# Layer 2's first stage in slots of one block product, part of its weight preparation in layer 1, and the last stage's sums on VectorE

## The chip, the cores and the metric

The kernel runs on one core of a Trainium2 chip. The metric is the device time of one execution in microseconds. The kernel before takes 1717.92 us, the median of three runs (1717.18 to 1718.33).

## The reference

Pooled attention is followed by two MLPs, all in float32; the second layer's product is where most of the change lies.

```python
k_p, v_p = k.mean over 8 rows, v.mean over 8 rows          # 8 batches, 8 heads, 576 x 64
x = softmax(q @ k_p.T / 8) @ v_p                            # -> 4608 tokens x 512
h = x @ w_in1;  y = (h * sigmoid(h)) @ w_out1               # 512 -> 2048 -> 512
h = y @ w_in2;  g = h * clip(h + 3, 0, 6) / 6;  out = g @ w_out2
```

## The kernel before

The 4608 tokens are cut into 9 groups of 512. The order of the instructions on every engine is the order in which the program issues them, and each engine works its queue in that order. All transfers between HBM and SBUF are issued by SP, in program order too.

**Layer 1 with attention** comes first: 9 groups of 16 steps, a step being one block of 128 hidden features (`h_mm`, then `y_mm` of the step before). Beside it the attention of the next group is computed, and the weights of layer 2 are prepared. Float32 products are made of three matmuls on a high part and a low part, so every operand is split: ScalarE makes the high part, GpSimd or VectorE the difference.

**Layer 2** uses a scheme of seven block products in place of eight. Both operands, cut into 2 x 2 blocks, are replaced by seven sums of blocks each. The *preparation* of a weight matrix is done in 8 pairs of feature blocks, and for each pair: four quarter blocks are loaded (`load_half`) and converted from their float64 words (`half_a`: one ScalarE and three VectorE instructions); GpSimd forms four sums (`combine`); seven results are split (`half_b`: ScalarE and GpSimd) and stored to HBM (`ws`). `factor_jobs(piece)` deals this out in seven jobs a pair. In layer 1 a job is begun in those steps of groups 1 to 7 for which `SPLITTING` has a one (9 of 16). There `w_in2` (piece 0) is prepared; `w_out2` (piece 1) is prepared in layer 2's first stage, by `work`, called at three of the seven products (at one of them every second time).

**The first stage of layer 2** walks over 36 values of `e` (9 groups of tokens times 4 double blocks of features). Each `e` has seven block products, numbered k, in the order 0, 4, 3 of the `e` before, 5, 2 of the `e` before, 1, 6; the first `e` has five and two are left at the end, 252 in all. A product is 12 matmuls of 256 columns (`product`, L639). Products 0, 5, 6 and 3 add up in one PSUM bank, 4 and 2 in another, and the running sum is read out in between (L1024, L1034 on ScalarE; L1027, L1039 on VectorE), so that TensorE cannot add product 5 before product 0 has been read. Four products of an `e` end in a *gate* (`relu6`): ScalarE's Relu (L654), then VectorE's minimum and product (L656) into a tile `go`, which is stored to HBM (`g2`, L658). The store is put on a list, `later`, and issued when the next `e` begins. `go` has four buffers. The seven sums of the next group's x are made by `make_x` (GpSimd sum, ScalarE high part, GpSimd low part), from four blocks that `load_x1` loads two `e` ahead.

In the last four `e`, `last_factor` loads the prepared blocks of `w_out2` (512 KB each, 28 in all) into places that the last products have freed, and `load_g` the first group's gates (8 of 512 KB).

**The last stage** has 9 groups of seven products of 48 matmuls each (`last_product`, L712). `sums` forms the sums of g on GpSimd (L206, `gr<-gr`, 8 of 1024 columns a group), `split_g` splits the next product's operand (ScalarE L698, VectorE L699), and the results are added up by `summed` (VectorE, L1063) and, twice a group, by `combine` on GpSimd.

Of the kernel before, what the change touches and what calls it, by code (L numbers as in the profile page):

```python
# [20 lines left out]
GT = 512  # L21
# [4 lines left out]
def kernel(  # L26
# [152 lines left out]
    def half_a(f, piece, a):  # L179
        raw = half_raw.pop((f, piece, a))  # L180
        hw = raw[:, :, 1]
        mag = prep_tile("mag", [P, HW], F32)
        bits = mag.bitcast(U32)
        nc.scalar.activation(mag, hw.bitcast(F32), AF.Copy, scale=2.0 ** -112)
# [11 lines left out]
        half_mag[f, piece, a] = mag  # L196

    def half_b(mag, dst):

        t = prep_tile("out", [P, 2, HW], F32R)  # L200
        nc.scalar.activation(t[:, 0], mag, AF.Copy)  # L201
        nc.gpsimd.tensor_tensor(out=t[:, 1], in0=mag, in1=t[:, 0].bitcast(F32), op=ALU.subtract)  # L202
# [12 lines left out]
    def pair_jobs(p, piece, rest):  # L215
        d, j = divmod(p, 2)
        f = 2 * p
        m = half_mag
        a11, a12, a21, a22 = (
            ((f, 0, 0), (f, 0, 1), (f + 1, 0, 0), (f + 1, 0, 1)),  # L220
            ((f, 1, 0), (f + 1, 1, 0), (f, 1, 1), (f + 1, 1, 1)),
        )[piece]
# [360 lines left out]
    def open_late():  # L583
# [3 lines left out]
        prep.update(raw=(own, "raw", 3), mag=(own, "mag", 4), out=(own, "out", 4))  # L587
# [20 lines left out]
    def make_x(g, i):  # L608

        k = MADE[i]  # L610
        b11, b12, b21, b22 = (x_raw[a, b] for a in range(2) for b in range(2))
        src = (b11, b11, b11, b12, b21, b21, b22)[i]
# [6 lines left out]
        elif i == 5:  # L619
            combine(ALU.subtract, b21, b21, b11)  # L620
        t = late["x"][(7 * g + i) % 9]
        nc.scalar.activation(t[:, 0], src, AF.Copy)  # L622
        nc.gpsimd.tensor_tensor(out=t[:, 1], in0=src, in1=t[:, 0].bitcast(F32), op=ALU.subtract)  # L623
        x_st[g, k] = t.rearrange("p a (c n) -> p a c n", c=2)
# [26 lines left out]
    def relu6(h, g, d, fh, th):  # L651

        t = new_f32("t", "t")
        nc.scalar.activation(t, h, AF.Relu, scale=1.0 / 6.0, bias=half)  # L654
        o = new_f32("o", "go")
        nc.vector.scalar_tensor_tensor(out=o, in0=t, scalar=1.0, in1=h, op0=ALU.min, op1=ALU.mult)  # L656
        dst = g2[g][:, fh, th, 2 * d:2 * d + 2, :]
        later.append(lambda: nc.sync.dma_start(out=dst, in_=o.rearrange("p (j n) -> p j n", j=2)))  # L658
# [19 lines left out]
    def sums(g, k):  # L678
# [3 lines left out]
        for dd in range(2):  # L682
            b11, b12, b21, b22 = (g_in[g, a, b, dd] for a in range(2) for b in range(2))
            if k == 4:
                combine(ALU.subtract, b11, b12, b11)
            elif k == 6:
                combine(ALU.subtract, b12, b22, b12)
            elif k == 5:
                combine(ALU.subtract, b11, b22, b11)
            else:  # L690
                combine(ALU.subtract, b21, b21, b11)
# [57 lines left out]
    with tc.manual_schedule():  # L749
# [100 lines left out]
        SPLITTING = (0, 1, 0, 1, 0, 1, 1, 1, 0, 1, 0, 1, 0, 1, 1, 0)  # L850
        jobs = list(factor_jobs(0))
# [105 lines left out]
        jobs = list(factor_jobs(1))  # L957
        ahead2 = [key for key, _ in jobs if key]
        jobs_b = []

        def work(n):

            nonlocal jobs_b
            for _ in range(n):
                for job in jobs_b:
                    job()
                jobs_b = []
                if jobs:
                    key, jobs_b = jobs.pop(0)
                    if key:  # L970
                        half_a(*key)
                    while ahead2 and len(half_raw) < 3:
                        load_half(*ahead2.pop(0))

        while len(half_raw) < 3:
            load_half(*ahead2.pop(0))
        n_all = NG * ND
        xs_, zs, kept = {}, {}, {}
        freed = []
        wanted = [(d, k) for k in LAST for d in range(ND)]  # L980

# [4 lines left out]
        for e in range(n_all + 1):  # L986
            g, d = divmod(e, ND)
            due, later[:] = list(later), []
            for job in due:
                job()  # L990
            if e == n_all - ND:
                while jobs or jobs_b:
                    work(1)
                for job in later:
                    job()
                later.clear()
# [3 lines left out]
            if n_all - ND < e:  # L1000
                while freed:
                    last_factor()
                for _ in range(4):
                    if g_next[0] < 10 and g_next[0] < 8:
                        n = g_next[0]
                        load_g(0, *G_ORDER[n // 2], n % 2)
            if g + 1 < NG and d == 1:
                load_x1(g + 1)
            for ee, k in steps_of(e, n_all):
                gg, dd = divmod(ee, ND)  # L1010
                if k == 0:
                    xs_[ee] = ps_h.tile([P, GT], F32, tag="h", name="px")
                elif k == 4:
                    zs[ee] = ps_a.tile([P, GT], F32, tag="a", name="pz")
                ps = {0: xs_, 5: xs_, 6: xs_, 3: xs_, 4: zs, 2: zs}.get(k, {}).get(ee)
                if ps is None:
                    ps = ps_y.tile([P, 512], F32, tag=f"y{ee % 2}", name="py")
                product(ps, gg, dd, k, k in (0, 4, 1))
                if gg == NG - 1:
                    freed.append(tag_of[0, dd, k])  # L1020
                ph = column_sets(ps)
                if k in (0, 5, 6):
                    t = kept[ee, k] = new_f32({0: "gh", 5: "gl"}[k], f"c{k}") if k != 6 else late["pool"].tile([P, GT], F32, tag="u3", name="u3")
                    nc.scalar.activation(in_sets(t), ph, AF.Copy)  # L1024
                    if k == 6:
                        u4 = late["pool"].tile([P, GT], F32, tag="u4", name="u4", bufs=1)
                        nc.vector.tensor_tensor(  # L1027
                            out=in_sets(u4), in0=in_sets(t), in1=column_sets(zs[ee]), op=ALU.add
                        )
                        kept.pop((ee, 6))  # L1030
                        relu6(u4, gg, dd, 1, 1)
                elif k == 3:
                    t = late["pool"].tile([P, GT], F32, tag="u3", name="u3")
                    nc.scalar.activation(in_sets(t), ph, AF.Copy)  # L1034
                    relu6(t, gg, dd, 1, 0)
# [130 lines left out]
```

## Time and profile before

| What | Value |
|---|---|
| Median of 3 runs | 1717.92 us |
| Profiled execution, its own time | 1716.91 us |
| Its span (first to last instruction) | 1715.0 us |
| Mean granted TensorE clock | 0.978 |
| TensorE matmul busy | 1591.8 us (93%) |
| VectorE, ScalarE, GpSimd busy | 1089.2, 702.2, 677.0 us |
| Attention and layer 1 | 0 to 887 us |
| First stage of layer 2 | 887 to 1356 us |
| Last stage | 1356 to 1715 us |

Times in the profile are in microseconds from the span's start; "mean ns" is the duration of one instruction. PE is TensorE, PEld its weight loads, DVE VectorE, ACT ScalarE, POOL GpSimd, SPq the queue of SP, which issues the transfers. An entry such as `go<-t,c` names the tile written and those read. `<-` before an engine or DMA names what ended an idle time.

### The profile page before, as it was taken

The page shows a single profiled execution, that of the slowest core. Times are in us where ns is not written, and L with a number is a line of the kernel's source. Part 1 is how long each engine was busy: PE and PEld are TensorE (multiplying, and loading weights), DVE is VectorE, ACT ScalarE, POOL GpSimd, SP SyncE. Part 2 cuts the span into 40 slices and gives each one's busy share as a digit, 9 for nine tenths or more (in the row PEclk, how much of TensorE's full clock was granted, in tenths as well). Part 3 has the DMA queues.
Part 4 walks back from the last instruction along what each step waited for, and adds up shares of the span by engine and source line. Part 5 has one row for each costly group of instructions (what it writes and reads, how often), then busy time and mean ns, then how long its engine had stood idle before and what let it go on. Part 6 is the DMA issues. An engine that isn't in the chain of part 4 may idle for free.

```text
span 1715.0 us, 26954 instructions
## 1 busy us (share of the span) xinstructions
PE 1591.8 (93%) x10510; PEld 1429.4 (83%) x10510; DVE 1089.2 (64%) x1457; ACT 702.2 (41%) x1208; POOL 677.0 (39%) x523
## 2 busy tenths in 40 slices
PE   7899999999999999999998776788998699999998
PEld 6466888888888888888898775778898699999998
DVE  7996655656656565544235545546444588888887
ACT  5443553333333333332235445455554334434333
POOL 4633441212121212100215345445332377767676
PEclk9999999999999999999999999989999899999999
DMA  9342333333334343212545453644335943344441
GB/s 294 140 153 72 113 109 120 124 125 110 109 97 140 111 139 110 94 51 87 211 161 173 167 178 121 216 166 166 142 130 227 381 130 123 125 138 132 146 146 47
DMA packets 119711, 245.42 MB, mean 143 GB/s; under 512 B 12448, under 2 KB 38944, under 8 KB 119584
## 3 DMA queue, kind: packets, MB, share of 16 engines
q1 hardware_dynamic: 119584, 243.71, 41.9%
q8 instruction: 82, 1.34, 0.3%
q14 instruction: 45, 0.37, 0.1%
HBM read 146.67 MB, written 96.99 MB: 142 GB/s over the span
## 4 chain that ended last, share of the span: by engine, by line
PE 56%; DVE 15%; issue 12%; POOL 7%; DMA 5%; ACT 5%; SPq 0%; POOLq 0%; ACTq 0%; DVEq 0%
PE hps L502 20%; PE y L560 20%; DVE gs L699 8%; PE pl L712 8%; PE px L639 2%; POOL xst L623 2%; POOL xr L206 2%; PE aps L467 2%; ACT t L654 2%; PE aps L363 2%; POOL hout L202 1%; DMA g<-go 1%; PE pz L639 1%; ACT gs L698 1%; PE y L543 1%
## 5 line engine op out<-in xcount | busy, mean ns | idle before, releaser
L502 PE MATMUL hps<-x,whl 128*128 128x512 f32 x1728 | 402.1, 382 | 4.2 <-POOL whl L155 2.1
L502 PEld LDWEIGHTS hps<-x,whl 128*128 128x128 f32 x1728 | 326.1, 189 | 56.2 <-issue 5.4
L712 PE MATMUL pl<-wst,gs 128*128 128x256 f32 x3024 | 348.0, 277 | 12.4 <-DVE gs L699 6.8
L712 PEld LDWEIGHTS pl<-wst,gs 128*128 128x128 f32 x3024 | 342.6, 193 | 17.9 <-DVE gs L699 12.3
L560 PE MATMUL y<-gh,whl 128*128 128x512 f32 x1024 | 310.1, 384 | 0.0
L699 DVE TENSOR_TENSOR gs<-gr,gs 128x1024 fp32r<-128x1024 f32 x126 | 282.6, 2287 | 23.4 <-ACT gs L698 23.4
L639 PE MATMUL px<-xst,wst 128*128 128x256 f32 x1728 | 227.8, 288 | 64.6 <-ACT u L1024 38.9
L639 PEld LDWEIGHTS px<-xst,wst 128*128 128x128 f32 x1728 | 211.6, 200 | 77.3 <-ACT u L1024 44.3
L202 POOL TENSOR_TENSOR hout<-hmag,hout 128x256 fp32r<-128x256 f32 x112 | 87.8, 784 | 460.7 <-ACT hout L201 436.7
L206 POOL TENSOR_TENSOR gr<-gr 128x1024 f32<-128x1024 f32 x72 | 238.8, 3351 | 63.0 <-DVE gs L699 57.2
L522 DVE SCALAR_TENSOR_TENSOR hps<-t,hps 128x512 f32<-128x512 f32 x128 | 88.3, 690 | 217.7 <-ACT t L521 217.3
L560 PEld LDWEIGHTS y<-gh,whl 128*128 128x128 f32 x1024 | 189.5, 189 | 29.6 <-issue 4.1
L521 ACT ACTIVATE t<-hps 128x512 f32<-128x512 f32 x128 | 76.4, 597 | 297.4 <-PE hps L502 295.8
L560 PE MATMUL y<-gl,whl 128*128 128x512 f32 x512 | 194.1, 379 | 0.0
L698 ACT ACTIVATE gs<-gr 128x1024 fp32r<-128x1024 f32 x126 | 127.4, 1055 | 147.8 <-PE pl L712 104.2
L623 POOL TENSOR_TENSOR xst<-xr,xst 128x512 fp32r<-128x512 f32 x63 | 81.3, 1292 | 255.3 <-ACT xst L622 172.3
L531 DVE TENSOR_TENSOR gl<-hps,gh 128x512 fp32r<-128x512 f32 x128 | 88.5, 691 | 86.0 <-ACT gh L530 86.0
L656 DVE SCALAR_TENSOR_TENSOR go<-t,u 128x512 f32<-128x512 f32 x72 | 54.6, 758 | 137.5 <-ACT t L654 76.0
L639 PE MATMUL pz<-xst,wst 128*128 128x256 f32 x864 | 117.1, 289 | 22.7 <-DVE c L1039 22.7
L639 PEld LDWEIGHTS pz<-xst,wst 128*128 128x128 f32 x864 | 109.5, 203 | 25.1 <-DVE c L1039 25.0
L530 ACT ACTIVATE gh<-hps 128x512 fp32r<-128x512 f32 x128 | 76.6, 599 | 115.4 <-DVE hps L522 115.4
L654 ACT ACTIVATE t<-c,half 128x512 f32<-128x512 f32 x72 | 52.0, 722 | 149.6 <-DVE c L1039 149.5
(104 smaller groups left out, 1783.5 us busy)
## 6 DMA issues: line engine op xcount, KB each, us to landing
g<-go SPq DMA_DIRECT2D x144, 256.0 KB
gr<-g SPq DMA_DIRECT2D x72, 512.0 KB
ws<-hout SPq DMA_DIRECT2D x112, 256.0 KB
wst<-ws SPq DMA_DIRECT2D x56, 512.0 KB
bl<-bT SPq DMA_DIRECT2D x28, 384.0 KB
x<-o SPq DMA_DIRECT2D x36, 256.0 KB
xr<-x SPq DMA_DIRECT2D x36, 256.0 KB
wraw<-in_moe_w_in_dram SPq DMA_DIRECT2D x16, 512.0 KB
```

Of the source, the lines that this page charges most:

```text
L202: nc.gpsimd.tensor_tensor(out=t[:, 1], in0=mag, in1=t[:, 0].bitcast(F32), op=ALU.subtract)
L206: nc.gpsimd.tensor_tensor(out=out, in0=a, in1=b, op=op)
L502: nc.tensor.matmul(ps, w[:, c, :], shuffled(x[:, c, :]), start=(c == 0 and n == 0), stop=(c == NKC - 1 and n == 2),)
L522: nc.vector.scalar_tensor_tensor(out=ps, in0=t, scalar=1.0, in1=ps, op0=ALU.add, op1=ALU.mult)
L531: nc.vector.tensor_tensor(out=in_two(gl), in0=dealt(ps), in1=in_two(gh).bitcast(F32), op=ALU.subtract)
L560: nc.tensor.matmul(ps, a, shuffled(b), start=(f == 0 and n == 0), stop=(f == NF - 1 and n == 2),)
L623: nc.gpsimd.tensor_tensor(out=t[:, 1], in0=src, in1=t[:, 0].bitcast(F32), op=ALU.subtract)
L639: nc.tensor.matmul(ps[:, j * HW:(j + 1) * HW], w[:, j, a, c, :], shuffled(x[:, b, c, :]), start=(first and j == 0 and n == 0 and c == 0), ...
L654: nc.scalar.activation(t, h, AF.Relu, scale=1.0 / 6.0, bias=half)
L698: nc.scalar.activation(t[:, dd, 0], src, AF.Copy)
L699: nc.vector.tensor_tensor(out=t[:, dd, 1], in0=src, in1=t[:, dd, 0].bitcast(F32), op=ALU.subtract)
L712: nc.tensor.matmul(ps[:, c * HW:(c + 1) * HW], t[:, dd, a, i, c * P:(c + 1) * P], shuffled(w[:, b]), start=(dd == 0 and c == 0 and i == 0 ...
```

## The change

**Layer 1.** `factor_jobs` takes no piece now: it deals out all 8 pairs of `w_in2` and then the first four (`EARLY`) of `w_out2`, 85 jobs in place of 57, and `SPLITTING` has 14 ones in 16.

**First stage of layer 2.** The loop runs over a flat list of the 252 products, called slots. The remaining four pairs of `w_out2` are cut into single steps (`pair_steps`: one conversion on ScalarE, one on VectorE, one high part, one low part, or one sum), 104 in all, and one step is issued in every second slot. `half_a` and `half_b` are cut in two for that. A gate of slot n issues its Relu in slot n + 1, its VectorE product in n + 2 and its store in n + 3, each behind that slot's own copy or add. The Relu writes straight into the tile that is stored, and this tile rotates over six buffers (two of tag `t`, four of tag `o`). The steps of `make_x` are dealt out over slots in the same way by a table, `XPLAN`, and `load_x1` is issued in the fourth slot of its `e`.

**Last stage.** The sums run on VectorE, behind the split of the next product's operand and no longer ahead of it, and so do the two additions a group that were left on GpSimd.

```diff
     def half_a(f, piece, a):
+        half_scale(f, piece, a)
+        half_bits(f, piece, a)
...
-    def factor_jobs(piece):
+    EARLY = 4
+    def factor_jobs():
         rest = []
-        for p in range(NF // 2):
-            yield from pair_jobs(p, piece, rest)
+        for piece, n in ((0, NF // 2), (1, EARLY)):
+            for p in range(n):
+                yield from pair_jobs(p, piece, rest)
...
+    def pair_steps(p, piece, last):
...
+        return [
+            scale(a22), *first, scale(a21), bits(a22), scale(a11), bits(a21), head(3, a22),
+            tail(3, a22), make(ALU.add, a22, a21, a22), bits(a11), scale(a12), head(4, a22),
...
+        ], [head(2, a22), tail(2, a22)]
...
-        prep.update(raw=(own, "raw", 3), mag=(own, "mag", 4), out=(own, "out", 4))
+        prep.update(raw=(own, "raw", 3), mag=(own, "mag", 5), out=(own, "out", 4))
...
-                combine(ALU.subtract, b11, b12, b11)      # and three more, in sums()
+            nc.vector.tensor_tensor(out=to, in0=a, in1=b, op=ALU.subtract)
...
-        SPLITTING = (0, 1, 0, 1, 0, 1, 1, 1, 0, 1, 0, 1, 0, 1, 1, 0)
+        SPLITTING = (0, 1, 1, 1, 1, 1, 1, 1, 1, 1, 1, 1, 0, 1, 1, 1)
...
+        slots = [(e, ee, k) for e in range(n_all + 1) for ee, k in steps_of(e, n_all)]
...
+        def gate(n, h, g, d, fh, th):
+            o = new_f32("too"[n_gates[0] % 3], "go")
...
+            at(n + 1, relu)
+            at(n + 2, product_of)
+            at(n + 3, store)
+
+        XPLAN = {
+            (2, 0): ("h", 0), (2, 1): ("t", 0), (2, 2): ("s", 1), (2, 4): ("h", 1), (2, 5): ("t", 1),
...
+            (4, 6): ("t", 5), (5, 0): ("h", 6), (5, 1): ("t", 6),
+        }
...
+            for job in coming.pop(n, ()):
+                job()
...
+            if d == 1 and pos == 3 and g + 1 < NG:
                 load_x1(g + 1)
...
+            if steps and n % 2 and e < n_all - ND:
+                steps.pop(0)()
...
         for n, (g, k) in enumerate(seq):
+            if n + 1 < n_last:
+                split_g(*seq[n + 1])
             if k in ADDS:
                 sums(g, ADDS[k])
-            if n + 1 < n_last:
-                split_g(*seq[n + 1])
...
-                combine(ALU.add, s42, s42, u2)
+                nc.vector.tensor_tensor(out=s42, in0=s42, in1=u2, op=ALU.add)
```

## Rows read from the trace of the kernel before

**Rows 1.** The page: TensorE's busy tenths in 40 slices of 42.9 us.

```profile
PE   7899999999999999999998776788998699999998
```

**Rows 2.** Busy time by stage: PE, PEld, DVE, ACT, POOL, clock, DMA share, GB/s.

```profile
166.00:887.00 721.00, 721.00 (x3789) 625.13 (x3788) 400.52 (x739) 251.78 (x476) 147.01 (x175) 1.00 0.36 119
887.00:1205.00 318.00, 249.33 (x1948) 238.16 (x1948) 172.94 (x255) 162.29 (x311) 149.39 (x147) 0.93 0.48 168
1205.00:1309.00 104.00, 98.34 (x844) 95.21 (x843) 51.45 (x70) 60.25 (x101) 40.01 (x32) 1.00 0.35 127
...
1310.00:1366.00 56.00, 37.15 (x283) 35.90 (x282) 24.36 (x28) 19.48 (x29) 8.44 (x3) 0.85 1.03 403
1356.00:1715.00 359.00, 348.02 (x3024) 342.58 (x3024) 310.04 (x171) 135.46 (x144) 262.00 (x90) 0.99 0.40 133
```

**Rows 3.** TensorE's weight loads in order of time: start, duration, tiles, count.

```profile
886.84 1.52 PEld L639 LDWEIGHTS px<-xst,wst 128*128 128x128 f32 x12
...
1309.76 1.42 PEld L639 LDWEIGHTS pz<-xst,wst 128*128 128x128 f32 x12
1311.10 1.42 PEld L639 LDWEIGHTS py<-xst,wst 128*128 128x128 f32 x12
```

**Rows 4.** The chain of work that ended last, from 1700 us: start, us, what.

```profile
1699.99 11.29 PE pl L712 x101
```

**Rows 5.** Who waited for whom, 890 to 1205 us: total, times, longest.

```profile
DVE go L656 <- DMA g<-go: 40.1, 11, 6.6
...
PE px L639 <- ACT u L1024: 27.9, 17, 2.3
...
PE pz L639 <- DVE c L1039: 20.8, 11, 4.3
PE px L639 <- ACT c L1024: 20.0, 24, 3.3
```

**Rows 6.** The same stretch, waits of SP's queue.

```profile
SPq L176 <- DVE hmag L192: 136.7, 22, 16.1
```

**Rows 7.** SP's issues in order of time, first stage of layer 2.

```profile
1227.38 1.95 SPq L603 DMA_DIRECT2D xr<-x  x4
...
1268.22 1.96 SPq L603 DMA_DIRECT2D xr<-x  x4
...
1309.06 2.39 SPq L252 DMA_DIRECT2D wst<-ws  x5
```

**Rows 8.** The end of the first stage in order of time; idle time before in brackets.

```profile
1325.32 0.69 DVE L656 SCALAR_TENSOR_TENSOR go<-t,u 128x512 f32<-128x512 f32 x1 [7.52 <-DMA g<-go]
...
1341.83 0.69 DVE L656 SCALAR_TENSOR_TENSOR go<-t,u 128x512 f32<-128x512 f32 x1 [9.52 <-DMA g<-go]
...
1353.18 0.69 DVE L656 SCALAR_TENSOR_TENSOR go<-t,u 128x512 f32<-128x512 f32 x1 [4.36 <-DMA g<-go]
...
1356.22 0.80 PE L712 MATMUL pl<-wst,gs 128*128 128x256 f32 x2 [5.39 <-ACT gs L698]
```

**Rows 9.** Busy time on the preparation's tile `hmag` by stage: DVE, ACT, POOL.

```profile
166.00:887.00 721.00, 47.51 (x96) 40.12 (x88) 63.90 (x88) 1.00 0.36 119
887.00:1205.00 318.00, 63.33 (x96) 34.60 (x88) 70.59 (x87) 0.93 0.48 168
```

**Rows 10.** VectorE's differences of the last stage: duration, min/median/max in ns.

```profile
L699 DVE TENSOR_TENSOR gs<-gr,gs x126: 1209/2070/3403, 1356.3 to 1703.6; 128x1024 fp32r<-128x1024 f32 x126
```

**Rows 11.** The last stage in order of time, around 1480 to 1511 us.

```profile
1478.03 23.29 POOL L206 TENSOR_TENSOR gr<-gr 128x1024 f32<-128x1024 f32 x7
1479.09 3.40 DVE L699 TENSOR_TENSOR gs<-gr,gs 128x1024 fp32r<-128x1024 f32 x1
...
1502.92 2.35 DVE L699 TENSOR_TENSOR gs<-gr,gs 128x1024 fp32r<-128x1024 f32 x2
1505.21 0.69 DVE L1063 TENSOR_TENSOR u<-c,pl 128x512 f32<-128x512 f32 x1
```

**Rows 12.** Who waited for whom, 1356 to 1715 us: total, times, longest.

```profile
PE pl L712 <- DVE gs L699: 6.8, 18, 0.5
```

More of the change, by code (lines that the diff above doesn't have):

```diff
@@ L606, with x_blocks, x_sum @@
     MADE = (0, 4, 5, 6, 1, 3, 2)
[L608 to L612, printed above, removed]
+    def x_blocks():
+        return [x_raw[a, b] for a in range(2) for b in range(2)]
+    def x_sum(i):
+        b11, b12, b21, b22 = x_blocks()
         if i == 1:
@@ L649, in new_f32, with late_f32 @@
         return p2.tile([P, GT], F32, tag=tag, name=name, bufs=4 if tag == "o" else 2)
[L651 to L658, printed above, removed]
+    def late_f32(tag, name, bufs=2):
+        return late["pool"].tile([P, GT], F32, tag=tag, name=name, bufs=bufs)
     G_ORDER = ((0, 0), (1, 0), (0, 1), (1, 1))
@@ L955 @@
         make_x(0, 6)
[L957 to L976, printed above, removed]
+        steps = []
+        last = []
+        for p in range(EARLY, NF // 2):
+            now, last = pair_steps(p, 1, last)
+            steps += now
+        steps += last
+        ahead2 = [
+            q[i] for p in range(EARLY, NF // 2) for q in (quarters(p, 1),) for i in (3, 2, 0, 1)
+        ]
         n_all = NG * ND
+        slots = [(e, ee, k) for e in range(n_all + 1) for ee, k in steps_of(e, n_all)]
         xs_, zs, kept = {}, {}, {}
@@ L984, in last_factor, with at, relu, product_of @@
             load_factor(1, d, k, freed.pop(0))
-        for e in range(n_all + 1):
-            g, d = divmod(e, ND)
[L988 to L996, printed above, removed]
+        def at(n, job):
+            coming.setdefault(n, []).append(job)
+        n_gates = [0]
+        def gate(n, h, g, d, fh, th):
+            o = new_f32("too"[n_gates[0] % 3], "go")
+            n_gates[0] += 1
+            def relu():
+                nc.scalar.activation(o, h, AF.Relu, scale=1.0 / 6.0, bias=half)
+            def product_of():
+                nc.vector.scalar_tensor_tensor(
+                    out=o, in0=o, scalar=1.0, in1=h, op0=ALU.min, op1=ALU.mult
+                )
+            def store():
+                nc.sync.dma_start(
+                    out=g2[g][:, fh, th, 2 * d:2 * d + 2, :], in_=o.rearrange("p (j n) -> p j n", j=2)
+                )
+            at(n + 1, relu)
+            at(n + 2, product_of)
+            at(n + 3, store)
+        XPLAN = {
[4 rows of a table added]
+        }
+        def x_job(what, g, i):
+            if what == "s":
+                x_sum(i)
+            elif what == "h":
+                x_head(g, i)
+            else:
+                x_tail(g, i)
+        while len(half_raw) < 3:
+            load_half(*ahead2.pop(0))
+        e_now, pos = -1, 0
+        n = -1
+        total = len(slots)
+        for n, (e, ee, k) in enumerate(slots):
+            g, d = divmod(e, ND)
+            e_now, pos = e, pos + 1 if e == e_now else 0
+            if pos == 0 and e == n_all - ND:
+                while steps:
+                    steps.pop(0)()
+                while later:
+                    later.pop(0)()
                 late["prep"].close()
@@ new lines @@
+            for job in coming.pop(n, ()):
+                job()
+            for of, q in ((d, g + 1), (d + ND, g)):
+                if (of, pos) in XPLAN and 0 < q < NG:
+                    what, i = XPLAN[of, pos]
+                    x_job(what, q, i)
+            if d == 1 and pos == 3 and g + 1 < NG:
+                load_x1(g + 1)
+            if steps and n % 2 and e < n_all - ND:
+                steps.pop(0)()
+                while ahead2 and len(half_raw) < 3:
+                    load_half(*ahead2.pop(0))
@@ L1052 @@
+            while later:
+                later.pop(0)()
+        for m in range(total, total + 4):
+            for job in coming.pop(m, ()):
+                job()
         while freed and wanted:
             last_factor()
-        for job in later:
-            job()
-        later.clear()
+        assert not coming and not wanted
         n_last = NG * 7
@@ L1111 @@
                 s4 = kept.pop("s4")
-                combine(ALU.add, s4, s4, u3)
+                nc.vector.tensor_tensor(out=s4, in0=s4, in1=u3, op=ALU.add)
                 store(g, 1, 1, s4)
```

160 lines of the change are left out of this document (93 added, 67 removed), and 2 rows, old and new, of the table XPLAN.

## The prediction

> **What bounds the kernel now.** I read the page's slices first, then busy times by stage, the waits of each stretch, and the timeline where a wait is long. In the slices TensorE is full in layer 1 and in the last stage, and has holes between, in the first stage of layer 2 [rows 1]. By stage: from 166 to 887 us TensorE is busy in all of the 721.0 us, and no other engine in more than 401. From 887 to 1205 us, while w_out2 is prepared, it is busy 249 of 318 us; from 1205 to 1309, preparation done, 98 of 104; from 1310 to 1366, 37 of 56; in the last stage 348 of 359 [rows 2].
>
> The price of one product without holes is the distance of two neighbours, 1311.10 - 1309.76 = 1.34 us, or 0.112 us a matmul [rows 3]. The last stage agrees: 11.29 / 101 = 0.112 [rows 4]. The first stage has 252 products, 337.7 us of work, and took 1356.2 - 886.8 = 469.4 [rows 3, 8]. So 131.7 us are to be had there at most, in three parts.
>
> (a) The preparation. TensorE waits there for sums to be read out: 27.9 + 20.0 us for ScalarE's copies, 20.8 for VectorE's adds [rows 5]. Neither engine is full, 162 and 173 of 318 us [rows 2]; they are late because their queues are in order. One chain stands out. SP waits 136.7 us in 22 goes, up to 16.1, for a conversion to free a raw buffer [rows 6]; the stores of gates queue behind it; so VectorE waits 40.1 us for a `go` buffer [rows 5], and the adds and Relus behind that wait for VectorE.
>
> (b) 1205 to 1309 us. A group of 28 products takes 1268.22 - 1227.38 = 40.84 us, and the next, up to 1309.06, the same [rows 7]: 1.459 a product, 0.12 over the price.
>
> (c) The hand-over from 1309. The DMA engines are saturated, 403 GB/s from 1310 to 1366 us, 22.6 MB [rows 2]. VectorE waits three times for a store that stands behind the loads, 7.52, 9.52 and 4.36 us [rows 8].
>
> **Layer 1, four pairs more.** This is half of what `hmag` shows for one weight matrix. At layer 1's prices, half of 47.5, 40.1 and 63.9: 24 us on VectorE, 20 on ScalarE, 32 on GpSimd [rows 9], with 16 loads and 28 stores. All are dealt out over 721 us in which ScalarE has 469 idle and GpSimd 574 [rows 2]; TensorE's work, without a gap there although 57 jobs already ran beside it, hides them. Price 0; without that cover, all of ScalarE's, +20.
>
> **The first stage, slots 0 to 228** (up to the 34th e, where the loads of w_out2 begin). They took 1309.06 - 886.84 = 422.2 us [rows 3, 7], 1.844 each. What is left per slot: on ScalarE 60.25 us in 104, or 0.845 per product of 1.459, and half of 34.6 over 229 slots, 0.08: 0.92. VectorE: 0.72 + 0.14 = 0.86. GpSimd: 0.56 + 0.15 = 0.71 [rows 2, 9]. All stay below 1.34, so if order alone made the holes, TensorE sets the pace. The order now has a copy ahead of a Relu whose add came a slot earlier, and every copy has two products' time, 2.7 us, before TensorE needs it. SP waits for at most one conversion just issued, and a gate's buffer comes round after six gates, some ten slots, 14 us, where the longest of the old waits was 6.6 [rows 5]. What is late next: the first block of x is loaded four slots, 5.4 us, before ScalarE wants it; its four loads are issued in 2 us [rows 7] and at 403 GB/s the 1.05 MB move in 2.6, so it just fits; then the last low part of x, on GpSimd, about a product ahead of its use. Bounds for the slot: 1.34, all holes gone, and 1.459, the old pace without preparation. I take 1.37, a quarter of the way, since what made 1.459 was order and the order is what is edited. 229 x 1.37 = 313.7: a gain of 108.5 us (bounds 115.3 and 88.1).
>
> **The hand-over.** Bytes and issue order of the loads stay: 9 loads of 512 KB, then 11, 7, 9. At 403 GB/s such a load takes 1.30 us, a store of 256 KB 0.65. This explains the old waits: 9 loads, four stores, 11 loads and a store are 11.7 + 2.6 + 14.3 + 0.65 = 29.3 us from 1310, or 1339.3; the wait ended at 1341.83 [rows 8], so a landing comes 2.5 us behind its turn. In the new order stores are issued one by one, three of the four of an e behind the next e's loads, and the wait moves from VectorE to ScalarE's Relu, which now writes the stored buffer; queued behind it are ScalarE's copies, and TensorE waits for those after three products. The last Relu's buffer is freed by the twelfth store: 27 loads and 12 stores, 35.1 + 7.8, with 1 us of start and 2.5 of landing 46.4 us after the loads begin. From the end of the old last wait to the last stage's first matmul it is 1356.22 - 1353.18 = 3.0 [rows 8]. So the last stage starts at about +49, against 1356.22 - 1309.06 = 47.2 now: no gain, +2. Two buffers more, and a place later in the queue, cancel. Bounds: 23 products at 1.34 and the old last idle time of 5.4 [rows 8], 36 us (-11), and +6 if the stalls add up.
>
> The Trainium skill, DMA: Bandwidth & Descriptors, section Queues, rings and completion order, says that completion is not in order of issue, so that a later transfer may finish first. By that the stores could pass the loads and the stage would end as TensorE does; the landing worked out above, 2.5 us behind its turn, shows no such passing.
>
> **The last stage.** VectorE's difference takes 1.21 us at least, 2.07 at the median, 3.40 at most [rows 10]. These are two states: beside GpSimd's sums one takes 3.40, about as long as one of those (23.29 / 7 = 3.33), and with GpSimd idle two take 2.35 [rows 11]. So a sum of this size (two SBUF operands) costs 1.21 on VectorE, and the differences fall to 1.21 too, because nothing is left on GpSimd. Per group: (14 + 8) x 1.21 + 7 x 0.69 [rows 11] = 31.4 us, against TensorE's 7 x 48 x 0.112 = 37.6. In the fullest product, two differences, two sums and an add, 5.5 us, stand against 5.4; the split goes first, so what slips is the sum. TensorE's work is 3024 x 0.112 = 338.7; from 1356.2 to 1711.3 [rows 4, 8] it took 355.1, so 16.4 us are holes: 18 waits for `gs` [rows 12] with the restarts around them, and a start at a mean granted clock below full (0.85 up to 1366 us [rows 2]). The waits go, 4 us of start stay: -12 (bounds -16, and 0 if late splits stay).
>
> The Trainium skill, Perfetto Trace Analysis, section Optimizing Scalar/DVE Operations, advises moving work from a saturated VectorE to others, even to GpSimd, and adds that this may not help, the two sharing an SBUF port. Its first half speaks against the edit, VectorE being busy 310 of 359 us; taken alone it makes the last rival below.
>
> **Sum.** 1715.0 - 108.5 + 2 - 12 + 0 = 1596.5 us of span. The runs' median is 2.9 above that span (the profiled execution's own time, 1716.91, 1.9), so **1599 us**.
>
> **Rivals.**
> 1. The old pace without preparation stays, 1.459: the x loads come late, or in-order waits return on ScalarE. 229 x 0.089 = +20: 1620. For it: ScalarE carries copies, Relus and high parts, and one slot may hold three. Against: two slots of slack.
> 2. The slots do little, and the preparation costs what it cost, by half. Its 318 us held 1948 / 12 = 162 products, so it cost (318 / 162 - 1.459) x 162 = 82 us; half is 41 over rival 1: 1661. For it: VectorE is slowed in the conversions by GpSimd (63.3 against 47.5 us on the same tile [rows 9]). Against: both have half their time free.
> 3. The hand-over runs as TensorE does, 36 us in place of 49: 1586.
> 4. Slower. VectorE becomes the last stage's bound, because a wide instruction keeps the old median of 2.07 us [rows 10]. Then 22 x 2.07 + 4.8 = 50.3 a group, 12.7 over TensorE, 115 in all: 1726 with the 12 not gained. The stage is VectorE's from (37.6 - 4.8) / 22 = 1.49 us on, and the whole slower than before from (119 - 12) / 198 = 0.54 more, 2.03. Against: the 1.21 is measured beside an idle GpSimd, and GpSimd is left with nothing.
>
> **Chances.** My forecast 0.62 (its own range 1585 to 1612), rival 1 0.16, rival 2 0.11, rival 3 0.07, rival 4 0.04. The range takes in the forecast, rivals 1 and 3 and their bounds, up to halfway to rival 2: 1582 to 1640, leaving out 0.15. A measurement of this kernel tells 0.2%, 3.4 us, from no change. Faster are the forecast and rivals 1 to 3, 0.95 with a hundredth kept for no change; same 0.01; slower 0.04.
>
> **What would show it.** Neighbouring products at 1.34 us through the first stage, no wait of VectorE for `go`, short waits of SP for conversions; the loads of w_out2 beginning near 1200; about 49 us from there to the last stage, DMA saturated, ScalarE waiting for `go`; L699 at 1.21 throughout, and a last stage near 347. It would be wrong if ScalarE waits for x, if TensorE waits for a late low part, if layer 1 ends after 890, or if L699 stays above 1.5.

## The result, and the profile after

The changed kernel takes 1605.84 us, the median of four runs (1605.65 to 1606.35); the kernel before, run beside it, takes 1717.55 us, the median of four (1717.16 to 1718.33). The ratio is 0.935, with a 95% interval of 0.9333 to 0.9366. The forecast was 1599 us, 6.8 below. The profiled execution of the changed kernel took 1605.65 us, its span 1603.5.

TensorE's slices on the page of the changed kernel, to be laid beside [rows 1]; a slice is 40.1 us now:

```profile
PE   7799999999999999999999999999998799999998
```

The row of 9s now runs from layer 1 through the first stage of layer 2. Between there and the end, the holes left are two slices at the hand-over. The busy times by stage of the changed kernel (columns as in [rows 2]): layer 1, the slots up to the first load of `w_out2`, the hand-over, the last stage.

```profile
154.00:903.00 749.00, 739.29 (x3826) 630.22 (x3825) 439.39 (x796) 268.50 (x526) 183.68 (x220) 1.00 0.39 130
903.00:1209.00 306.00, 306.00 (x2740) 305.92 (x2739) 202.81 (x273) 200.83 (x359) 155.31 (x132) 1.00 0.51 178
1209.00:1257.00 48.00, 34.23 (x290) 33.55 (x289) 18.60 (x30) 19.98 (x34) 2.56 (x2) 0.90 1.01 391
1257.00:1603.00 346.00, 341.37 (x3024) 340.88 (x3024) 269.44 (x262) 135.04 (x144) 0.00 (x0) 0.99 0.42 140
```

In the first stage TensorE is busy in all of 306.0 us at a granted clock of 1.00, where it had 249.33 of 318 us at 0.93 [rows 2]. Layer 1 has lost what it had before, a TensorE without a gap: 9.7 of 749 us are missing. In the last stage it is busy 341.37 of 346.

The boundaries are read in the timeline of the changed kernel: TensorE's weight loads, SP's first load of `w_out2`, and the waits of ScalarE's Relu in the hand-over.

```profile
903.31 1.52 PEld L707 LDWEIGHTS px<-xst,wst 128*128 128x128 f32 x12
...
1103.08 1.42 PEld L707 LDWEIGHTS pz<-xst,wst 128*128 128x128 f32 x12
1104.42 1.42 PEld L707 LDWEIGHTS py<-xst,wst 128*128 128x128 f32 x12
...
1209.64 2.34 SPq L303 DMA_DIRECT2D wst<-ws  x5
...
1225.88 0.72 ACT L1047 ACTIVATE go<-u,half 128x512 f32<-128x512 f32 x1 [3.96 <-DMA g<-go]
...
1243.25 0.72 ACT L1047 ACTIVATE go<-u,half 128x512 f32<-128x512 f32 x1 [11.95 <-DMA g<-go]
...
1254.62 1.33 ACT L1047 ACTIVATE go<-u,half 128x512 f32<-128x512 f32 x2 [3.71 <-DMA g<-go]
...
1257.57 0.80 PE L770 MATMUL pl<-wst,gs 128*128 128x256 f32 x2 [6.01 <-ACT gs L756]
```

Neighbouring products stand 1104.42 - 1103.08 = 1.34 us apart. The boundaries that the forecast used cut both spans into stretches that add up:

| Stretch | Before | After | Measured | Forecast |
|---|---|---|---|---|
| Start to the end of layer 1 | 886.84 | 903.31 | +16.5 | 0 |
| To SP's first load of `w_out2` | 422.2 | 306.3 | -115.9 | -108.5 |
| Hand-over, to the last stage's first matmul | 47.2 | 47.9 | +0.8 | +2 |
| Last stage | 358.8 | 345.9 | -12.9 | -12 |
| Span | 1715.0 | 1603.5 | -111.5 | -118.5 |

The boundary between slots and hand-over is SP's, not TensorE's, and it does not lie at the same product in both kernels: the load stands in SP's queue behind stores of gates. By it TensorE had run 1948 + 844 = 2792 matmuls in the kernel before [rows 2], nearly 233 products, and 2740 in the changed kernel, 228. Cut at the first matmul of TensorE's own 230th product, the first 229 products (2748 matmuls, and one more at the edge) take, in the kernel before and in the changed kernel:

```profile
887.05:1303.47 416.42, 342.60 (x2749) 328.70 (x2748) 221.02 (x320) 219.38 (x405) 189.03 (x178) 0.95 0.45 159
903.52:1210.39 306.87, 306.87 (x2749) 306.86 (x2748) 203.58 (x273) 201.27 (x360) 155.74 (x133) 1.00 0.51 178
```

So a slot went from 1.818 to 1.340 us, -109.5 us in all, and the hand-over from 1356.22 - 1303.47 = 52.8 to 1257.57 - 1210.39 = 47.2, -5.6. Their sum is that of the table. From here on, slots and hand-over are cut in this way.

Two more readings answer to [rows 6] and [rows 10]. First, from the changed kernel's view of waits, SP's wait for a conversion from 887 to 1200 us (total, times, longest):

```profile
SPq L176 <- DVE hmag L199: 33.9, 12, 5.9
```

Second, the changed kernel's differences and sums on VectorE in the last stage (minimum, median and maximum in ns):

```profile
L757 DVE TENSOR_TENSOR gs<-gr,gs x126: 1215/1219/1226, 1257.6 to 1591.3; 128x1024 fp32r<-128x1024 f32 x126
L749 DVE TENSOR_TENSOR gr<-gr x72: 1217/1220/1224, 1262.2 to 1583.1; 128x1024 f32<-128x1024 f32 x72
```

The wait of 136.7 us is down to 33.9, and the three durations of a difference have become one, 1.22 us, which a sum costs too.

### The profile page after: what moved, and what is told of

It is laid out like the page before. It is cut to its first block, busy times and chain, and to the rows that moved or that the text cites. A ratio compares the mean times of both kernels' runs of the same rounds, so it can differ in the third digit from the quotient of the medians.

```text
span 1603.5 us, 27104 instructions
## 1 busy us (share of the span) xinstructions
PE 1554.1 (97%) x10510; PEld 1402.0 (87%) x10510; DVE 1063.3 (66%) x1547; ACT 695.6 (43%) x1208; POOL 419.2 (26%) x433
## 4 chain that ended last, share of the span: by engine, by line
PE 78%; DVE 11%; DMA 4%; ACT 3%; issue 3%; POOL 1%; SPq 0%; DVEq 0%; ACTq 0%; POOLq 0%
PE pl L770 21%; PE y L611 17%; PE hps L553 16%; PE px L707 11%; PE pz L707 5%; PE py L707 3%; PE aps L518 1%; DMA wst<-ws 1%; DMA g<-go 1%; PE y L594 1%; PE aps L414 1%; DVE hps L573 1%; ACT gh L581 1%; DVE wmag L120 1%; DVE wmag L117 1%
## 5 line engine op out<-in xcount | busy, mean ns | idle before, releaser
L770 PE MATMUL pl<-wst,gs 128*128 128x256 f32 x3024 | 341.4, 277 | 6.5 <-ACT gs L756 6.0
L707 PE MATMUL px<-xst,wst 128*128 128x256 f32 x1728 | 206.6, 277 | 8.3 <-ACT c L1118 7.6
L573 DVE SCALAR_TENSOR_TENSOR hps<-t,hps 128x512 f32<-128x512 f32 x128 | 88.1, 688 | 183.7 <-ACT t L572 183.5
L707 PEld LDWEIGHTS px<-xst,wst 128*128 128x128 f32 x1728 | 200.2, 193 | 8.9 <-ACT c L1118 7.8
L757 DVE TENSOR_TENSOR gs<-gr,gs 128x1024 fp32r<-128x1024 f32 x126 | 148.4, 1220 | 26.0 <-ACT gs L756 26.0
L611 PEld LDWEIGHTS y<-gl,whl 128*128 128x128 f32 x512 | 96.9, 189 | 19.2 <-DVE gl L582 6.1
L707 PE MATMUL pz<-xst,wst 128*128 128x256 f32 x864 | 108.3, 276 | 0.0
L707 PEld LDWEIGHTS pz<-xst,wst 128*128 128x128 f32 x864 | 102.3, 192 | 0.0
L749 DVE TENSOR_TENSOR gr<-gr 128x1024 f32<-128x1024 f32 x72 | 84.8, 1220 | 0.0
L1050 DVE SCALAR_TENSOR_TENSOR go<-go,u 128x512 f32<-128x512 f32 x72 | 64.6, 899 | 21.0 <-ACT go L1047 20.1
```

Source lines behind the costliest of these rows:

```text
L573: nc.vector.scalar_tensor_tensor(out=ps, in0=t, scalar=1.0, in1=ps, op0=ALU.add, op1=ALU.mult)
L611: nc.tensor.matmul(ps, a, shuffled(b), start=(f == 0 and n == 0), stop=(f == NF - 1 and n == 2),)
L707: nc.tensor.matmul(ps[:, j * HW:(j + 1) * HW], w[:, j, a, c, :], shuffled(x[:, b, c, :]), start=(first and j == 0 and n == 0 and c == 0), ...
L749: nc.vector.tensor_tensor(out=to, in0=a, in1=b, op=ALU.subtract)
L757: nc.vector.tensor_tensor(out=t[:, dd, 1], in0=src, in1=t[:, dd, 0].bitcast(F32), op=ALU.subtract)
L770: nc.tensor.matmul(ps[:, c * HW:(c + 1) * HW], t[:, dd, a, i, c * P:(c + 1) * P], shuffled(w[:, b]), start=(dd == 0 and c == 0 and i == 0 ...
```

## The experiments

Two things were open: why layer 1 became longer, and which part of the change gave the slots their 109.5 us. In the table a slot is the mean of the first 229 products, with their sum behind it, and the hand-over runs from there to the last stage's first matmul. The expectations below still cut at SP's load: what they call 1.338, 47.9 and 35.2 is 1.340, 47.2 and 34.4 here. Runs without an interval are one execution each, with the profile; the kernel before took 1715.5 to 1719.4 us beside them.

| Run | Time | Layer 1 ends | A slot | Hand-over | Last stage |
|---|---|---|---|---|---|
| before | 1717.55 | 886.84 | 1.818 (416.4) | 52.8 | 358.8 |
| after | 1605.84 | 903.31 | 1.340 (306.9) | 47.2 | 345.9 |
| a_f15 | 1592.51 | 891.05 | 1.342 (307.4) | 47.3 | 344.7 |
| a_f4 | 1602.07 | 900.86 | 1.340 (306.9) | 47.1 | 345.3 |
| h_hold | 1591.26 | 890.39 | 1.340 (306.9) | 47.4 | 344.2 |
| o_five | 1590.10 | 888.46 | 1.340 (307.0) | 47.1 | 345.5 |
| b_early0 | 1593.19 | 884.27 | 1.376 (315.1) | 47.1 | 344.7 |
| p_half_old | 1674.27 | 890.43 | 1.613 (369.3) | 52.9 | 358.9 |
| c_no_delay | 1644.03 | 903.72 | 1.510 (345.7) | 47.0 | 345.6 |
| d_pool_sums | 1616.14 | 900.95 | 1.340 (306.9) | 47.3 | 359.0 |
| t_throttle | 1591.17 | 902.62 | 1.342 (307.4) | 34.4 | 344.6 |

The end of layer 1 carries up to 5 us of chance from the program's start (the first step of group 1 begins between 154.0 and 159.0 us in the runs of this document), so its length is better read from the first step of group 1 to the first step of group 8, against the kernel before: +18.6 us in the changed kernel.

### Layer 1: where the 16.5 us are

Each group from 2 to 7 loses 1.9 to 3.8 us, at the same places: in group 4, 1.9 us between the starts of steps 1 and 3, and 0.8 between those of steps 6 and 7. The timeline of the changed kernel at the beginning of that group, on VectorE, SP and TensorE:

```profile
445.52 0.68 DVE L624 TENSOR_SCALAR o<-y 128x512 f32<-128x512 f32 x1
446.60 3.23 SPq L627 DMA_DIRECT2D x<-o  x4
448.79 0.69 DVE L624 TENSOR_SCALAR o<-y 128x512 f32<-128x512 f32 x1 [2.58 <-ACT t L572]
449.54 0.70 PE L611 MATMUL y<-gh,whl 128*128 128x512 f32 x2 [0.31 <-DVE o L624]
449.92 0.38 SPq L215 DMA_DIRECT2D ws<-hout  x1
...
452.49 0.67 DVE L573 SCALAR_TENSOR_TENSOR hps<-t,hps 128x512 f32<-128x512 f32 x1
453.84 0.70 PE L611 MATMUL y<-gh,whl 128*128 128x512 f32 x2 [0.80 <-ACT gh L581]
```

L624 is `y_out`: the finished group's y is copied into four tiles of tag `o`, two on ScalarE, two on VectorE, and each is stored at L627. VectorE's second copy starts 2.58 us after VectorE was free. The wait is put down to ScalarE here; the view of waits, from 200 to 900 us, puts five of the six such waits down to a store of `y_out` itself:

```profile
DVE o L624 <- DMA x<-o: 12.9, 5, 2.6
```

Tag `o` has four buffers, and the preparation's split results (`hout`) are tiles of the same tag. A job begun in step 15 is split in step 0 of the next group, ahead of `y_out`; its result is put on `later` and is stored only in step 1, at 449.92. So `y_out` has three buffers for four tiles, and its fourth waits until the first one's store, issued at 446.60, has landed. Behind the copy stand VectorE's norm, its transposes and its product for the next h (L573, 452.49); ScalarE splits what that makes, and TensorE waits for it (0.80 us before 453.84). The old `SPLITTING` began no job in step 15. Rival causes were the step-4 job, beside the pooling of k, and simply more work than the cover holds. Four edits tell them apart.

**a_f15 and a_f4** take the job out of step 15, and out of step 4.

```diff
-SPLITTING = (0, 1, 1, 1, 1, 1, 1, 1, 1, 1, 1, 1, 0, 1, 1, 1)
+SPLITTING = (0, 1, 1, 1, 1, 1, 1, 1, 1, 1, 1, 1, 0, 1, 1, 0)   # a_f15
+SPLITTING = (0, 1, 1, 1, 0, 1, 1, 1, 1, 1, 1, 1, 0, 1, 1, 1)   # a_f4
```

> The changed kernel with SPLITTING's last one (step 15) set to zero: 13 jobs a group, 91 places for 85 jobs. In the changed kernel layer 1 ends 16.5 us later than before; the loss falls at steps 1 to 3 (1.9 us a group) and 4 to 7 (about 1 us a group), in groups 2 to 7. Theory A (buffers): a job begun at step 15 stores its split result in step 0 of the next group into a buffer of tag o, of which y_out needs all four just then; so y_out's copy waits 2.6 us on VectorE for that store, and the attention's work behind it makes the next h late. Then 10 to 12 us come back: 1594 to 1596, layer 1 ending near 892. Theory B (load): VectorE has too much to do in these steps whatever the buffers; then one job of 14 less gives back 1 to 2 us: 1604.

> The changed kernel with SPLITTING's one at step 4 set to zero, step 15 left. Theory A: the loss at steps 1 to 3 stays; that at steps 4 to 7 (a conversion at step 4 that is slowed by GpSimd and stands ahead of the pooling of k and of the next h on VectorE) goes: 4 to 6 us come back, 1600 to 1602. Theory B: 1 to 2 us, spread over the steps: 1604.

Without step 15, groups 1 to 7 are 2.3 us longer than before, not 18.6; without step 4, 13.7. So the job of step 15 carries 16 us and that of step 4 five, which overlap a little. The two copies of `y_out` now run back to back in a_f15's timeline of the same place, and VectorE's product for the next h follows 4.3 us after their start, not 7.0. TensorE has no gap, and the pair of matmuls that takes 0.70 us behind each of its two waits above takes 0.59 here; so a wait costs more than its idle time:

```profile
443.94 1.28 DVE L624 TENSOR_SCALAR o<-y 128x512 f32<-128x512 f32 x2
...
448.23 0.67 DVE L573 SCALAR_TENSOR_TENSOR hps<-t,hps 128x512 f32<-128x512 f32 x1
...
450.71 0.59 PE L611 MATMUL y<-gh,whl 128*128 128x512 f32 x2
```

**h_hold** begins the same jobs, and only leaves the split out of step 0, so that it runs in step 1.

```diff
-                    for job in jobs_b:
-                        job()
-                    jobs_b = []
+                    if f:
+                        for job in jobs_b:
+                            job()
+                        jobs_b = []
```

> The changed kernel with SPLITTING as changed (a job at step 15 too), but in step 0 of a group the split of the job before is not issued; it follows in step 1, after y_out has taken its four buffers of tag o. Theory A (buffers): the loss at steps 1 to 3 goes, as it went with the job at step 15 left out: layer 1 ends 8 to 14 us earlier, 1592 to 1598. Rival (a conversion at step 15 or simply 14 jobs are too many): layer 1 keeps at least half of its loss, 1599 to 1606.

**o_five** changes no order: tag `o` has five buffers, for its other uses too (tag `u3` gives one up for the room).

```diff
-    prep = {"raw": (att, "wmag", 4), "mag": (att, "hmag", 4), "out": (p2, "o", 4)}
+    prep = {"raw": (att, "wmag", 4), "mag": (att, "hmag", 4), "out": (p2, "o", 5)}
...
-            o = p2.tile([P, 512], F32, tag="o", name="o", bufs=4)
+            o = p2.tile([P, 512], F32, tag="o", name="o", bufs=5)
```

> The changed kernel with five buffers of tag o in place of four, nothing else in layer 1 altered (for the room, the tile u3 of layer 2's first stage has one buffer in place of two). In the changed kernel VectorE's fourth copy of y waits for the first copy's own store to x1 (by the waits five of six times a DMA x<-o), since the split result begun at step 15 holds one of the four buffers until step 1. If that is the whole cause at steps 1 to 3, a fifth buffer removes it with all jobs and their order as they are: layer 1 ends at 890 to 892 and the run takes 1590 to 1593. If the work of the job at step 15 costs something too, layer 1 ends later, up to 903. The slots of the first stage stay at 1.338, or grow by up to 0.05 if u3's single buffer is felt.

Groups 1 to 7 are 5.2 us longer than before in h_hold and 4.4 in o_five, with every job of the change in both. In o_five's view of waits from 200 to 900 us the wait for a store is gone; the only two of `y_out` on VectorE are for TensorE's product, at the end of layer 1:

```profile
DVE o L624 <- PE y L611: 1.8, 2, 1.2
```

One buffer explains 14.1 of the 18.6 us: the work itself was covered, the place to put it was not. My expectation for a_f15 held that the fourth copy waits for the store of `hout`; the trace names an x store. The missing buffer is the same, but not which store ends the wait.

### The first stage: order or work

**b_early0** undoes the layer-1 part alone: no pair of `w_out2` in layer 1, the old `SPLITTING`, and one of 208 steps in nearly every slot.

```diff
-    EARLY = 4
+    EARLY = 0
...
-            if steps and n % 2 and e < n_all - ND:
+            if steps and e < n_all - ND:
```

> The changed kernel with nothing of w_out2 in layer 1: EARLY = 0, SPLITTING as before, and all eight pairs (208 steps) in the first stage of layer 2, one step in every slot. Theory C (order made the holes): the slots stay at 1.34 us with the double load, since ScalarE, VectorE and GpSimd still have time left (about 1.0, 1.0 and 0.9 of 1.34 us a slot), and layer 1 ends at 887 again: 1587 to 1592. Theory D (load made them): each slot's preparation costs TensorE time as in the kernel before, 41 us for the half that is moved back, against 16.5 regained in layer 1: about 1630.

**p_half_old** does that part alone: the kernel before, with four pairs of `w_out2` in layer 1 and none of them begun in step 15.

```diff
...
-        SPLITTING = (0, 1, 0, 1, 0, 1, 1, 1, 0, 1, 0, 1, 0, 1, 1, 0)
-        jobs = list(factor_jobs(0))
+        SPLITTING = (0, 1, 1, 1, 1, 1, 1, 1, 1, 1, 1, 1, 0, 1, 1, 0)
+        jobs = list(factor_jobs(((0, 0, NF // 2), (1, 0, EARLY))))
...
```

> The kernel before with the first part of the change alone: four pairs of w_out2 prepared in layer 1 (13 jobs a group, none at step 15), the other four in the first stage as before, by jobs, no slots, no delays; last stage as before. If the preparation's price goes by its amount, 41 of its 82 us go, less 2 to 4 in layer 1: 1680. If the price is that of the rate at which jobs are issued (unchanged: as many a product, over half the stretch), the same 41 us. If SP's waits alone made it, more than half may stay: up to 1700. The changed kernel without this part took 1593, so with slots it is worth nothing.

In the old order half the preparation is worth 416.4 - 369.3 = 47.1 us of slots. In the new order it is worth 315.1 - 306.9 = 8.2: neither the nothing of Theory C nor the 41 of Theory D, and less than the 18.9 that layer 1 takes for it (in b_early0, groups 1 to 7 are 0.4 us shorter than before). This is why b_early0, with twice the preparation in the stage, is 12.7 us faster than the changed kernel. The new order by itself, with the whole preparation in the stage, gives 416.4 - 315.1 = 101.3 of the 109.5.

**c_no_delay** keeps the slots and takes the delays away: a gate's Relu, product and store are issued in the gate's own slot.

```diff
-            at(n + 1, relu)
-            at(n + 2, product_of)
-            at(n + 3, store)
+            at(n, relu)
+            at(n, product_of)
+            at(n, store)
```

> The changed kernel, but a gate's Relu, VectorE product and store are issued in the gate's own slot, as before the change; buffers, slots and the cut preparation stay. Theory F (the delays hold the pace): the Relu waits on ScalarE for an add of the same slot and stands ahead of the next copy; the slot goes back toward 1.459, between 1.40 and 1.46, 15 to 28 us: 1620 to 1634. Theory G (the cutting of the preparation into small steps holds it): the slot stays below 1.36: 1604 to 1611.

It lost 38.2 us, more than the 14 to 28 that I had allowed it. Its first 229 products:

```profile
903.94:1249.63 345.69, 322.06 (x2749) 315.02 (x2748) 202.57 (x274) 200.99 (x359) 155.42 (x132) 0.99 0.45 158
```

VectorE, ScalarE and GpSimd are busy as long as in the changed kernel (203.58, 201.27 and 155.74 us), but the slots are 345.7 - 306.9 = 38.8 us longer, which is the whole loss. TensorE is idle for 345.69 - 322.06 = 23.6 us and takes 322.06 - 306.87 = 15.2 longer over the same matmuls. The waits of c_no_delay from 905 to 1250 us:

```profile
ACT go L1047 <- DVE c L1131: 102.6, 65, 4.4
ACT go L1047 <- DVE u L1122: 35.4, 32, 3.9
PE px L707 <- ACT c L1118: 12.2, 14, 2.9
PE px L707 <- ACT u L1118: 10.7, 7, 2.1
```

ScalarE stands 138 us in front of Relus whose add VectorE has just begun, with the next bank's copy queued behind; TensorE then waits for that copy, and the two lines of it, 22.9 us, are nearly all of its idle time. Of the 15.2 us the clock explains 5 at most: it was granted at 0.50, the lower of its two levels, for 3.4 us from 1082.0 and for 6.8 from 1191.3. The other 10 would fit what layer 1 showed, matmuls that take longer behind a wait (0.70 for 0.59 us a pair); that was not traced further.

The delays thus carry 38.8 of the 101.3 us of the new order. The three of them were taken away together, and how the other 62 us divide between the cut preparation, the six buffers for gates in place of four, and the stores and steps of x issued by slots was not tried.

### The last stage and the hand-over

**d_pool_sums** puts the sums and the two additions back on GpSimd and keeps the new order, the split first.

```diff
-            nc.vector.tensor_tensor(out=to, in0=a, in1=b, op=ALU.subtract)
+            combine(ALU.subtract, to, a, b)
...
-                nc.vector.tensor_tensor(out=s42, in0=s42, in1=u2, op=ALU.add)
+                combine(ALU.add, s42, s42, u2)
```

> The changed kernel with the last stage's sums and its two additions a group back on GpSimd, the order of issue left as changed. Theory E (the port decides): L757's differences go back from 1.22 us to a median near 2 with two levels, 1.2 and 3.4, and the stage takes 10 to 14 us more than its 346: 1616 to 1619. Rival (the order of split and sums decides, not the engine): the stage stays within 3 us: 1605 to 1609.

The last stage is back at 359.0 us, 358.8 before, so the order alone gives nothing and the engine all of the 13. The differences on VectorE have their old durations again:

```profile
L757 DVE TENSOR_TENSOR gs<-gr,gs x126: 1209/2065/3406, 1255.4 to 1602.7; 128x1024 fp32r<-128x1024 f32 x126
```

**t_throttle** issues the same loads in the last four `e`, not in a burst at the head of each, but one at a time in two slots of three, so that no store stands behind a whole burst; what has no place there by then is loaded in the last stage.

```diff
-            if pos == 0 and e > n_all - ND:
-                while freed:
-                    last_factor()
-                for _ in range(4):
+            if e > n_all - ND and n % 3:
+                if g_next[0] < 8 and len(wanted) <= 24:
...
+                    load_g(0, *G_ORDER[i // 2], i % 2)
+                elif freed:
+                    last_factor()
```

> The changed kernel, but the loads of the last four e are issued one at a time in two slots of three (four blocks of w_out2, then the eight of g, then w_out2 again; what is left follows the last store), in place of 9, 11 and 7 at once ahead of the stores. Theory H (the hand-over of 47.9 us is set by stores that stand behind loads in the queue): ScalarE's waits for go of 19.6 us go, the hand-over is 36 to 40 us, and the last stage, 345.9 us, keeps its time, its blocks arriving at 1.3 us each against four per 5.4 us: 1594 to 1599. Rival (the bytes set it: the last stage only waits for what was put off): the hand-over shortens, but the last stage grows by as much: 1603 to 1608.

The hand-over falls from 47.2 to 34.4 us. No Relu waits for a store any more. The timeline of t_throttle, on SP and TensorE:

```profile
1209.51 0.38 SPq L303 DMA_DIRECT2D wst<-ws  x1
...
1244.67 0.30 PEld L770 LDWEIGHTS pl<-wst,gs 128*128 128x128 f32 x2 [2.67 <-ACT gs L756]
...
1245.16 20.53 SPq L303 DMA_DIRECT2D wst<-ws  x20
```

And the busy times of t_throttle in the same stretch:

```profile
1209.00:1245.00 36.00, 32.83 (x291) 32.42 (x290) 19.11 (x31) 21.14 (x35) 2.55 (x2) 1.00 0.94 337
```

The DMA engines are still nearly full (0.94), but TensorE runs at a granted clock of 1.00, where the burst left 0.90. And 20 of the 36 loads are issued after the last stage has begun at 1244.68, where the changed kernel left two (at 1262.71). The last stage is no longer for it (344.6): the rival, by which it grows by what is put off, did not come, and most of the burst was not needed that early. Two things were changed at once, then, the order and the bytes ahead of the last stage (337 GB/s in 36 us are 12.1 MB, 391 in 48 were 18.8); how the 12.8 us divide between them was not tried.

### The two findings together

Each of three versions deals the loads out and avoids the collision in `o`: **g1** by holding the split (h_hold), **g2** by no pair of `w_out2` in layer 1 (b_early0), **g3** by three pairs there, no job in steps 0, 4, 12 and 15, and a step in two slots of three.

> The two repairs together: the split held back in step 0, and the loads of the last four e dealt out one at a time. They lie in different stretches, so their gains add if the causes are right: layer 1 to 890.4, 229 slots of 1.338, 35.2 of hand-over, 344.5 of last stage, and 2 us around the span: 1579. If the hand-over's gain hangs on when it begins, or the last stage gives it back, 1585 or more.

> Nothing of w_out2 in layer 1 (a step of its preparation in every slot), and the loads dealt out: layer 1 to 885 or 887, 229 slots of 1.374, 35.2, 344.5, and 2 around: 1581 to 1583. Against the run with the split held back it tells whether half of the preparation in layer 1 is worth anything once its collision is gone: by the slots 8 us gained, by layer 1 about 4 to 6 paid, so 2 to 4 us at most.

> Three pairs of w_out2 in layer 1 with 12 jobs a group (none at steps 0, 4, 12 and 15), the other five in the first stage, a step in two slots of three, and the loads dealt out. If the two places of loss in layer 1 are the job at step 15 and the one at step 4, layer 1 ends about 888; 229 slots between 1.338 and 1.36: 1576 to 1583.

| Run, 4 timed executions each | Median (lowest to highest) | Ratio to before | Layer 1 ends | A slot | Hand-over |
|---|---|---|---|---|---|
| g1_hold_throttle | 1578.75 (1576.32 to 1581.36) | 0.92 [0.9184, 0.9216] | 893.55 | 1.340 | 34.4 |
| g2_early0_throttle | 1580.18 (1579.05 to 1582.56) | 0.9212 [0.9195, 0.9228] | 883.98 | 1.371 | 34.4 |
| g3_early3_throttle | 1577.08 (1576.56 to 1578.41) | 0.9191 [0.9178, 0.9205] | 888.06 | 1.349 | 34.4 |

All three beat the changed kernel by 26 to 29 us, about the sum of the two repairs (14 and 12.8). Among themselves they differ by 0.2%, and their intervals overlap: none can be called the best.

## Why the prediction was right, and where it was off

**Sign, size and cause were right**: faster by 6.5% where 6.9% was forecast, within the range of 1582 to 1640, and by the stretches that the forecast named. Two terms were mis-sized, layer 1 by 16.5 us one way and the slots by 7 the other; that the sum came within 7 us is in part luck.

**Layer 1, "Price 0", is the step that failed.** It measured +16.5, near the upper bound that the text had set for it (+20), and the sign of error named in the text, a layer 1 that ends after 890, came up (903.31). But the cover of engine time, on which that bound rested, was not what gave way: with a fifth buffer the same 28 jobs cost 4.4 us (o_five). The step counted the work, the loads and the stores, and not the tiles in which results lie until their stores are issued. What the view could have told: `hout` and `y_out`'s `o` are one tag with four buffers, `y_out` needs all four at once, and the new `SPLITTING` has a one in step 15.

**The slots** were taken at 1.37 us, between 1.34 and 1.459. They measured 1.340, the lower bound: 7 us better. One reading was wrong: the text found 229 products in the 422.2 us of the kernel before, where there were nearly 233 (2792 matmuls [rows 2]), so the old slot was 1.818 and not 1.844, and 5.6 us that it counted under the slots belong to the hand-over. The sum is not touched by it. The reasoning, that order and not load made the holes, holds in the main: with the whole preparation in the stage a slot takes 1.376 in the new order (b_early0), and with half of it 1.613 in the old one (p_half_old). Order here takes in the gates' two buffers more, which no run parts from it. The quarter that was kept back for late loads of x and low parts was not needed: no wait for x is among those of the changed kernel's slots, where TensorE is busy 306.87 of 306.87 us. The first load of `w_out2` came at 1209.64 and not near 1200 because layer 1 ended late.

**The hand-over** was worked out as a queue, at 1.30 us a load and 0.65 a store with landings 2.5 us behind their turn: the last Relu's buffer free 46.4 us after the loads begin, and 3.0 more to the last stage. Measured: 1254.62 - 1209.64 = 45.0, and 2.95. The wait moved from VectorE's product to ScalarE's Relu, as said. That the change gains nothing here (+2) is right only from SP's load on; from the same product it gained 5.6 us, 52.8 to 47.2, and what gave them was not tried (without the delays they stay: 47.0 in c_no_delay). The Trainium skill, DMA: Bandwidth & Descriptors, section Queues, rings and completion order, allows a later transfer to finish first; here ScalarE still waited 3.96, 11.95 and 3.71 us for stores behind loads, so no passing that would help was seen.

**The last stage** measured -12.9 for -12, the differences 1.22 for 1.21, and TensorE is idle 4.6 us of it, near the 4 that were left in the sum. The Trainium skill, Perfetto Trace Analysis, section Optimizing Scalar/DVE Operations, says that moving work from a saturated VectorE to GpSimd may make sense, and that it might not help, since the two share an SBUF read port. d_pool_sums moved the sums that way and lost the 13 us, so the second half fits this case: a difference takes 1.22 us with GpSimd idle and up to 3.41 beside its sums. That the port is the reason is the skill's; the trace shows only that a difference is slower beside a sum.

**The rivals.** Rivals 1 and 2 (1.459 a slot; the preparation's price kept by half) did not come: 1.340. Rival 2's price is real in the old order: p_half_old gains 47.1 us of slots where the 41 of rival 2 were worked out for half. Rival 3 (a hand-over of 36 us) did not come here, but its time can be had: from SP's load, 1244.68 - 1209.51 = 35.2 us with the loads dealt out. Rival 4 (VectorE the bound of the last stage) did not come: no difference took over 1.23 us.

**Still open.** What the order of the first stage gives beside the delays (62 us); how the gain of the dealt-out loads divides between their order and the 18 that were put off; and what of layer 1's remaining 2 to 5 us is the step-4 job. a_f4 says five with the collision present; in g3, with no job in steps 4 and 15 and one pair less, groups 1 to 7 are only 0.5 us longer than before, but step 4 was not taken out by itself.

## What to carry to other kernels

Before work is moved under the cover of a full engine, list the buffers that it holds until its deferred stores are issued and who else needs that tag at that time; idle engine time alone is no cover. In queues that work in order, a dependent instruction issued one slot later, behind the next independent one, can be worth more than less work: 38.8 us of slots here, where taking half the preparation out gave 8.2. Where loads in bursts fill the DMA engines, deal them out and put off those that the next stage does not need at once, so that the small stores on which compute waits do not stand behind a burst. And when two kernels are compared by stretches, cut both at the same piece of work: SP's load came four products later in one than in the other.

## What was not expected of the hardware

DMA engines that are nearly full need not hold TensorE up: at a share of 0.94, with the loads dealt out, it was busy 32.83 of 36 us, where at 1.01, in bursts, it was busy 34.23 of 48. And holes cost more than their length. The granted clock of the first stage rose from 0.93 [rows 2] to 1.00 once TensorE had no holes; 0.07 x 318 = 22 us is the most that this can be of the 109.5. TensorE's idle time in the 229 products was 416.42 - 342.60 = 73.8 us, so the other 35.7 (342.60 - 306.87) are the same matmuls taking longer, by the clock and behind each wait.
